# Three kernels in one program: where scratch stores, weight loads and token groups stand in the order

## Chip, cores and metric

One core of one Trainium2 chip. The metric is the time of the whole program on the device in microseconds (us), median of several runs. The profile is of one execution, taken by the hardware profiler.

## What is computed

An attention with a learned position bias, then a mixture of experts with one expert per token, then a gated feed-forward layer; 4 batches of 576 tokens, model width 512. Cut to what matters here:

```python
# attention: 4 batches x 8 heads, 576 positions, 64 channels, bias from a small net of log distances
attn = softmax(q @ k.T / 8 + bias);  x = attn @ v                     # (2304, 512)
# experts: each token goes to the expert with the largest logit
e = argmax(x @ w_gate);  h = relu(x @ w1[e]);  x = gate * (h @ w2[e]) # 8 experts, 512 -> 1024 -> 512
# gated layer, 512 -> 1536 -> 512
g = x @ w_gate2;  out = (g * sigmoid(g) * (x @ w_val)) @ w_out
```

## The kernel before

All of it is one program, and the order of the instructions on each engine is written out by hand; an engine's queue, and SP's queue of DMA issues too, is worked off in order. Matmuls are done in pairs of halves (a high part and the rest), so every weight and every activation is split by a copy on ScalarE and a subtraction on VectorE.

The attention ends at about 300 us. Then come 64 steps, numbered 0 to 63, 16 for each batch: step s of a batch does one block of 128 hidden units for one half of the tokens (the loop over `16 * B`, L1161). A step n issues on TensorE the first product of step n + 1 (`h_step`, L590, followed by a relu on ScalarE, L592, and a difference on VectorE, L593) and then the second product of step n (`y_step`, L603). So the relu of a step has about one step of time before TensorE needs it. After these two come all tasks noted for step n: `at(n, ...)` puts a task in the list `todo[n]`, `after(n, ...)` one in `done[n]`, and `todo[n]` is issued before `done[n]`.

The tasks that matter here:

- **Expert weights.** A batch b, from 1 on, has n = 16b - 15 as its base. Its expert's eight blocks come in three loads (`m_load`, `load_w`, L534 for w1 and L535 for w2) at steps n + 7, n + 8 and n + 11, that is 8, 9, 12 for batch 1, 24, 25, 28 for batch 2 and 40, 41, 44 for batch 3. The first two hold three blocks each, 768 KB for w1 and 768 KB for w2. `m_conv` splits block f at step n + 9 + f (`conv_w`, L551 on ScalarE, L553 on VectorE): block 0 at 10, 26 and 42.
- **Pieces of the last layer's weights.** The weights of the last layer lie in HBM as 64-bit numbers. A piece of them is fetched (`fetch_w`, L974 and L976, 512 KB), made 32-bit by one pass on ScalarE (L985) and three on VectorE (L988, L991, L994), and stored to the scratch tensor `wn` in HBM (L1031, 256 KB). 18 such pieces are done in the steps of the list `NS`. Piece i is fetched three steps before its own (`stash_ld`), into one of three buffers, and converted into one of two halves of `xT2`: `s_out(i)` is the half i % 2. So a piece may be converted only when the store of piece i - 2 has left. The steps of `NS2` divide a conversion over two steps. The store is noted by `after` for the step behind the conversion.
- **Batch list.** At steps 39 to 42 small products sort what is left over (`rest_list`, L516 the last), and 43 to 63 prepare one small extra group of tokens.

The last layer, from about 570 us, takes 36 iterations: three token groups j (768 tokens each, 384 and 384 side by side), and for each 12 blocks f of 128 hidden units, the middle group backwards. Iteration n does products for block f into the banks X and Y (L1276 in the first six iterations, L1267 after), VectorE's and ScalarE's work between, and the output product of iteration n - 1 (`outs`, L1529). In iterations 1 to 5 further pieces of weights are converted (`n_tasks`, L985 to L994, store L1413) and fetched again (`n_load`). Group j's x is read by `ld_x(j)` (L1468, and for the last group also L1479, whose rows are 128 bytes) into the tile `xr`, and its sums (L1233) are made by VectorE: those of the first read in iterations 3 and 4, those of the others in the third and second last iteration of the group before. `ld_x(0)` stands at the end of iteration 2, `ld_x(1)` at the end of iteration 7 and `ld_x(2)` at the end of iteration 18. Group 0 and group 1 are parts of the first three batches in an order known at run time; group 2 is the last batch and the last 64 tokens of each batch, whose outputs are stored in pieces of 32 rows. At the end of a group the six output tiles are copied (VectorE for m = 0 and 2, ScalarE for m = 1, the last tile half and half) and stored (L1548). In the last group the stores of m = 1, and half of the 32-row stores, are issued by ScalarE's queue, the others by SP.

Of the kernel before, what the change touches and what calls it, by code (L numbers as in the profile page):

```python
# [9 lines left out]
F32 = mybir.dt.float32  # L10
# [25 lines left out]
PR = {0: 72, 1: 73, 5: 75}  # L36
EB = 4
N0, NPL = 6, 6
NS = (9, 10, 13, 18, 19, 20, 21, 24, 25, 26, 29, 34, 35, 37, 39, 40, 41, 43)
NS2 = (13, 29, 37, 43)  # L40
RT = (3, 4, 5, 5, 6, 7, 7)
QN = (43, 46, 44, 46, 49, 54, 56)
# [71 lines left out]
def body(tc, qt, kt, va, vb, ws, moe_w_gate, moe_w_output_gate, moe_w1, moe_w2, w_gate, w_val, w_out, ctab, cst, cst2, out):  # L114
    nc = tc.nc
    with ExitStack() as ctx:
# [4 lines left out]
        vw = ctx.enter_context(tc.tile_pool(name="vw", bufs=1))  # L121
# [34 lines left out]
        for r in range(4):  # L156
            o = slice(32 * r, 32 * r + 32)
# [9 lines left out]
        vt = {}  # L167
# [594 lines left out]
        mu = [dict(raw=[], ws={}, xs={}) for b in range(B)]  # L762
# [3 lines left out]
        def m_load(b, gi):  # L766
            if gi == 0:
                mu[b]["e"] = nc.values_load(e0i[0:1, b:b + 1], engines=[ENG.SP], min_val=0, max_val=7)
            mu[b]["raw"] += load_w(mu[b]["e"], gi, "rv" if (b, gi) == (0, 1) else "vt")

        def m_load_f(b, f):

# [103 lines left out]
        for cnt in range(Z0):  # L876
            z_iter()
            n = -(-len(extra) // (Z0 - cnt))
# [13 lines left out]
        for n, (ui, c) in enumerate(steps):  # L892
            p, b = units[ui]
# [120 lines left out]
        def s_out(i):  # L1014
            return xT[2][:, 512 * (i % 2):512 * (i % 2) + 512]

        def stash(i, n, m, two):

            def cv(k, e):
                for f in fs()[k:e]:  # L1020
                    f()
            fl = []

            def fs():
                if not fl:
                    fl.extend(narrow_w(s_raw(i), s_out(i)))
                return fl
            at(m, lambda: cv(0, 4 if not two else 3))
            if two:
                at(m + 1, lambda: cv(3, 4))  # L1030
            after(m + 1 + two, lambda: nc.sync.dma_start(wn[n], s_out(i)))  # L1031

        def stash_ld(i, n, m):
            at(m - 3, lambda: fetch_w(n, s_raw(i)))
# [3 lines left out]
        def after(n, *fs):  # L1038
            done.setdefault(n, []).extend(fs)
# [327 lines left out]
        with ExitStack() as c2:  # L1367
# [152 lines left out]
            def outs(n, h, m):  # L1520
                j, f = steps[n]
                first, last = n % NF == 0, n % NF == NF - 1
                if first:
                    ops[h, m] = po.tile([128, 512], F32, tag=f"o{h}{m}", name="o")
                t = ops[h, m]
                uh, ul = (u[:, 128 * m:128 * m + 128] for u in sv[n]["u"][h])
                oh, ol = wt[f][2]
                for i, (u, w) in enumerate(((uh, oh), (uh, ol), (ul, oh))):
                    nc.tensor.matmul(t, u, w, start=first and i == 0, stop=last and i == 2)  # L1529
                if last:  # L1530
                    end = j == 2
                    if end:
                        o = sv["end"][:, 512 * (3 * h + m):512 * (3 * h + m) + 512]
                    else:
                        o = wp.tile([128, DM], F32, tag="ot", bufs=3, name="ot")
                    parts = rows(j, h, m)
                    if end and (h, m) == (1, 2):
                        nc.vector.tensor_copy(o[:, 0:256], t[:, 0:256])
                        nc.scalar.activation(o[:, 256:512], t[:, 256:512], AF.Copy)
                        nc.sync.dma_start(parts[0][2][:, 0:256], o[:, 0:256])  # L1540
                        nc.scalar.dma_start(parts[0][2][:, 256:512], o[:, 256:512])
                        return
                    if m % 2 == 0:
                        nc.vector.tensor_copy(o, t)
                    else:
                        nc.scalar.activation(o, t, AF.Copy)
                    for a, c, dst in parts:
                        (nc.scalar if end and (m % 2 or a >= 64) else nc.sync).dma_start(dst, o[a:a + c])  # L1548

            def it(n):  # L1550

# [28 lines left out]
                if n < NPL:  # L1580
                    st_new(n, X, Y, {t: wp.tile([128, TH], F32, tag=t, bufs=2, name=t) for t in ("c1", "c2")})
                    s = sv[n]
                    F("a")
                    plain(0, 0, f, X)
                    p_silu(s, 0)
                    F("b")
                    O(0, 0)
                    plain(0, 1, f, Y)
                    p_mul(s, 0)
                    u_hi(s, 0)  # L1590
                    F("c")
                    u_lo(s, 0)
                    O(0, 1)
                    O(0, 2)
                    F("d")
                    plain(1, 0, f, X)
                    p_silu(s, 1)
                    F("e")
                    O(1, 0)
                    O(1, 1)  # L1600
                    F("f")
                    plain(1, 1, f, Y)
                    p_mul(s, 1)
                    u_hi(s, 1)
                    F("g")
                    u_lo(s, 1)
                    O(1, 2)
                    F("h")
                    if i == 2:
                        ld_x(0)  # L1610
                    return
                st_new(n, X, Y, {t: wp.tile([128, TH], F32, tag=t, bufs=1 + (t[0] == "c"), name=t) for t in ("x1", "u2", "u4", "c1", "c2", "c3")})
# [36 lines left out]
                F("h")  # L1649
                O(1, 2)  # L1650
                if j < 2 and i == NPL + (j == 0):
                    ld_x(j + 1)

            for n in range(6, 9):
                n_load(n)
# [23 lines left out]
```

## Time and profile before

| | us |
|---|---|
| median of 3 runs | 1004.45 |
| lowest and highest | 1001.57, 1006.0 |
| the profiled execution, own time | 1007.01 |
| its span, first to last instruction | 1005.1 |

Busy time is the time in which an engine executed; TensorE's matmuls overlap, so a busy TensorE is not one at its peak, and the count of matmuls in a stretch says more. The granted clock is the share of full speed that TensorE got: 1.00 is 2.4 GHz, 0.5 is 1.2 GHz. In a timeline each row has start, duration, engine, line, operation, output and inputs, and how often it came; in square brackets stands the idle time before it and what ended it. SPq and ACTq are the queues of DMA issues; their durations are those of issuing, not of moving bytes.

### The profile page before, as it was taken

What the parts mean: (1) busy time and instruction counts of PE and PEld (TensorE: products, weight loads), DVE (VectorE), ACT (ScalarE), POOL (GpSimd) and SP (SyncE); (2) the same over time, 40 slices, a digit from 0 to 9 for tenths busy, and PEclk for the clock granted to TensorE, in tenths of its full rate; (3) what the DMA queues carried; (4) which work ended last, traced back from release to release, by engine and by line L of the source; (5) the groups of instructions that cost most, each with busy time, mean ns of one, the idle gap of its engine ahead of it and who ended that gap; (6) DMA issues with size and microseconds to landing.
All of it is one profiled execution on the core that took longest, in us unless ns stands there. A gap on an engine that the chain in (4) does not pass through costs nothing. (4 is left out here: it accounts for less than half of the span.)

```text
span 1005.1 us, 19647 instructions
## 1 busy us (share of the span) xinstructions
PE 959.9 (96%) x7633; PEld 819.7 (82%) x7633; DVE 694.7 (69%) x1548; ACT 531.3 (53%) x1125; POOL 115.8 (12%) x116
## 2 busy tenths in 40 slices
PE   7979999999999999797999998999999999999997
PEld 2337777777668999796999897999999999999996
DVE  8967788777786576574656666867636677556673
ACT  6767777777775252341434542554534554444542
POOL 2673333343300000000000000000000000000000
PEclk9998999999999999798999999999999999999999
DMA  6774324333044465766646367241122420302211
GB/s 205 206 247 151 117 86 151 99 116 111 2 141 155 158 232 160 257 198 215 203 163 214 131 211 240 94 127 32 41 86 64 126 63 1 126 32 63 64 32 63
DMA packets 88639, 130.26 MB, mean 130 GB/s; under 512 B 13632, under 2 KB 46400, under 8 KB 88544
## 3 DMA queue, kind: packets, MB, share of 16 engines
q1 hardware_dynamic: 87920, 128.07, 40.2%
q8 instruction: 60, 0.98, 0.4%
q10 hardware_dynamic: 624, 0.92, 0.3%
q14 instruction: 35, 0.29, 0.1%
HBM read 93.50 MB, written 35.46 MB: 128 GB/s over the span
## 5 line engine op out<-in xcount | busy, mean ns | idle before, releaser
L272 DVE CUSTOM_DVE_ANT_0 E<-S,bias 128x576 f32<-128x576 f32 x128 | 91.8, 755 | 34.8 <-PE S L268 26.5
L277 ACT ACTIVATE E<-E,st 128x576 f32<-128x576 f32 x144 | 110.3, 769 | 4.2 <-DVE st L272 3.9
L1267 PE MATMUL Y<-fv,ws 128*128 128x384 f32 x540 | 108.8, 336 | 0.0
L1267 PEld LDWEIGHTS Y<-fv,ws 128*128 128x128 f32 x540 | 95.7, 188 | 3.0 <-issue 0.2
L268 PEld LDWEIGHTS S<-kh,qz 64*128 64x128 f32 (+1 forms) x576 | 57.7, 189 | 38.7 <-DVE st L272 21.0
L379 PE MATMUL pv<-pt,rawv 128*64 128x320 f32 (+1 forms) x576 | 88.1, 423 | 0.0
L268 PE MATMUL S<-kh,qz 64*128 64x288 f32 (+1 forms) x576 | 83.9, 326 | 4.0 <-DVE st L272 2.6
L1529 PE MATMUL o<-ws,u 128*128 128x512 f32 x306 | 84.2, 395 | 0.0
L592 ACT ACTIVATE qz<-T 128x288 fp32r<-128x288 f32 x63 | 25.8, 409 | 94.7 <-PE T L590 94.5
L1008 DVE TENSOR_TENSOR ws<-r,ws 128x512 fp32r<-128x512 f32 (+1 forms) x66 | 51.4, 779 | 31.9 <-ACT ws L1005 30.9
L1267 PE MATMUL X<-fr,ws 128*128 128x384 f32 x360 | 73.4, 339 | 0.0
L318 ACT ACTIVATE pt<-T 128x512 f32<-128x512 f32 (+3 forms) x112 | 50.7, 467 | 40.4 <-PE T L295 40.0
L1267 PEld LDWEIGHTS X<-fr,ws 128*128 128x128 f32 x360 | 65.0, 188 | 5.6
L603 PE MATMUL y<-qz,w2hl 128*128 128x288 f32 x384 | 58.7, 302 | 8.6 <-ACT qz L592 6.1
L603 PEld LDWEIGHTS y<-qz,w2hl 128*128 128x128 f32 x384 | 54.3, 193 | 10.3 <-ACT qz L592 7.8
L1529 PEld LDWEIGHTS o<-ws,u 128*128 128x128 f32 x306 | 56.2, 188 | 6.6 <-DVE u L1322 0.4
L590 PE MATMUL T<-xh,whl 128*128 128x288 f32 x256 | 58.1, 303 | 0.0
L320 DVE COPY pt<-T 128x512 f32<-128x512 f32 (+3 forms) x112 | 55.8, 521 | 3.3 <-PE T L295 3.1
L593 DVE SCALAR_TENSOR_TENSOR qz<-T,qz 128x288 fp32r<-128x288 f32 x63 | 28.7, 455 | 42.0 <-ACT qz L592 41.4
L590 PE MATMUL T<-xh,w1hl 128*128 128x288 f32 x248 | 56.9, 305 | 0.0
L603 PE MATMUL y<-qz,whl 128*128 128x288 f32 x384 | 56.5, 296 | 0.0
L295 PE MATMUL T<-ident,E 64*128 64x64 f32 x1248 | 55.3, 225 | 0.0
(314 smaller groups left out, 2131.5 us busy)
## 6 DMA issues: line engine op xcount, KB each, us to landing
raww<-in_moe_w_dram SPq DMA_DIRECT2D x16, 768.0 KB, 7.3
r<-wn SPq DMA_DIRECT2D x22, 512.0 KB, 3.7
bscr<-ob SPq DMA_DIRECT2D x36, 288.0 KB, 3.3
bias<-bscr SPq DMA_DIRECT2D x14, 576.0 KB, 4.2
ro<-wn SPq DMA_DIRECT2D x22, 256.0 KB, 2.7
rawq<-in_qt_dram SPq DMA_DIRECT2D x16, 320.0 KB, 2.9
rawk<-in_kt_dram SPq DMA_DIRECT2D x16, 288.0 KB, 3.5
x<-xT SPq DMA_DIRECT2D x16, 288.0 KB, 4.8
```

The costliest lines, as they stand in the source:

```text
L268: nc.tensor.matmul(t[:, f, 0:288], x[k, a], y[k, o], start=i == 0, stop=i == 2)
L272: nc.vector.tensor_tensor_reduce(out=E.rearrange("p (a b) -> p a b", a=2), in0=ps[:, :, 0:288], in1=bt[p, hh, c].rearrange("p (a b) -> p a ...
L277: nc.scalar.activation(E, E, AF.Exp, bias=st[:, 2 * c + hh:2 * c + hh + 1], scale=-1.0, accum_out=st[:, 10 + 2 * c + hh:11 + 2 * c + hh])
L295: nc.tensor.transpose(t[r][:, at:at + 64], E[k, o:o + 128], ident[k, k])
L318: nc.scalar.activation(o, x, AF.Copy)
L320: nc.vector.tensor_copy(o, x)
L379: nc.tensor.matmul(st["ps"][64 * hh:64 * hh + 64, 0:w], vt[p][:, hh, b, c, :], y, start=c == order[0], stop=c == order[4])
L590: nc.tensor.matmul(ps, wa[:, x, k], xs[k][y][:, o], start=k == 0 and i == 0, stop=k == 3 and i == 2)
L603: nc.tensor.matmul(hbuf["y"][d // 2][:, d % 2, 0:288], wb[:, x, d], t[:, y:y + 288], start=f == 0 and i == 0, stop=(one or f == 7) and i == 2)
L1008: return lambda: eng.tensor_tensor(l, t, h.bitcast(F32), ALU.subtract)
L1267: nc.tensor.matmul(bank, a[:, c], x[:, k], start=first and k == 0 and n == 0, stop=k == 1 and n == 2, skip_group_check=True)
L1529: nc.tensor.matmul(t, u, w, start=first and i == 0, stop=last and i == 2)
```

## The change

Five edits. In `NS` the piece at step 26 is taken out and one at 49 is added, so that the pieces from the tenth on move to the next later place of the list. A piece's store is noted for the step in which its conversion ends, not for the one after. A batch's first weight load is issued as block 0 of w1 and of w2, and then blocks 1 and 2 of each. `ld_x(0)` stands at the end of iteration 1. The second and third group of tokens change places: the group with the 32-row pieces is loaded second and stored at iteration 24, and the whole blocks come last; all of the last stores are issued by SP.

```diff
-NS = (9, 10, 13, 18, 19, 20, 21, 24, 25, 26, 29, 34, 35, 37, 39, 40, 41, 43)
+NS = (9, 10, 13, 18, 19, 20, 21, 24, 25, 29, 34, 35, 37, 39, 40, 41, 43, 49)
@@ m_load
             if gi == 0:
                 mu[b]["e"] = nc.values_load(e0i[0:1, b:b + 1], engines=[ENG.SP], min_val=0, max_val=7)
-            mu[b]["raw"] += load_w(mu[b]["e"], gi, "rv" if (b, gi) == (0, 1) else "vt")
+                t, e = vw.tile([128, 3072], F32, tag="vt", bufs=2, name="raww"), mu[b]["e"]
+                a = t[:, 0:1536].rearrange("p (k f) -> p k f", k=4)
+                c = t[:, 1536:3072].rearrange("p (f d) -> p f d", f=3)
+                for i, j in ((0, 1), (1, 3)):
+                    nc.sync.dma_start(a[:, :, 128 * i:128 * j], moe_w1[bass.ds(e, 1), :, 128 * i:128 * j].rearrange("o (k p) f -> p (o k) f", p=128))
+                    nc.sync.dma_start(c[:, i:j], moe_w2[bass.ds(e, 1), 128 * i:128 * j].rearrange("o (f p) d -> p (o f) d", p=128))
+                mu[b]["raw"] += [(a[:, :, 128 * i:128 * i + 128], c[:, i]) for i in range(3)]
+            else:
+                mu[b]["raw"] += load_w(mu[b]["e"], gi, "rv" if (b, gi) == (0, 1) else "vt")
@@ stash
-            after(m + 1 + two, lambda: nc.sync.dma_start(wn[n], s_out(i)))
+            after(m + two, lambda: nc.sync.dma_start(wn[n], s_out(i)))
@@ outs
-                    parts = rows(j, h, m)
+                    parts = rows((0, 2, 1)[j], h, m)
                     if end and (h, m) == (1, 2):
...
-                        nc.scalar.dma_start(parts[0][2][:, 256:512], o[:, 256:512])
+                        nc.sync.dma_start(parts[0][2][:, 256:512], o[:, 256:512])
...
-                        (nc.scalar if end and (m % 2 or a >= 64) else nc.sync).dma_start(dst, o[a:a + c])
+                        nc.sync.dma_start(dst, o[a:a + c])
@@ it
-                    if i == 2:
+                    if i == 1:
                         ld_x(0)
...
-                    ld_x(j + 1)
+                    ld_x(2 - j)
```

## Rows read from the trace of the kernel before

**Rows 1.** The page, busy us and share of the span: TensorE.
```profile
PE 959.9 (96%) x7633; PEld 819.7 (82%) x7633; DVE 694.7 (69%) x1548; ACT 531.3 (53%) x1125; POOL 115.8 (12%) x116
```
**Rows 2.** Stretches: us, busy time (instructions) per engine, granted clock, DMA share, GB/s.
```profile
340.00:360.00 20.00, 18.68 (x139) 18.23 (x138) 13.15 (x24) 9.44 (x19) 0.00 (x0) 1.00 0.77 264
360.00:400.00 40.00, 40.00 (x318) 38.69 (x317) 30.04 (x73) 15.43 (x34) 0.11 (x1) 1.00 0.57 178
400.00:420.00 20.00, 13.31 (x76) 12.75 (x76) 7.07 (x14) 5.85 (x13) 0.00 (x0) 0.74 0.84 296
460.00:480.00 20.00, 13.04 (x92) 12.55 (x92) 7.84 (x26) 4.43 (x9) 0.00 (x0) 0.83 0.66 215
570.00:610.00 40.00, 40.00 (x220) 37.96 (x219) 27.11 (x48) 16.97 (x32) 0.00 (x0) 1.00 0.68 222
610.00:630.00 20.00, 15.94 (x75) 14.39 (x75) 12.19 (x20) 6.03 (x12) 0.00 (x0) 0.91 0.65 210
630.00:990.00 360.00, 360.00 (x1873) 334.99 (x1872) 237.66 (x431) 169.79 (x327) 0.00 (x0) 1.00 0.22 66
```
**Rows 3.** Timeline of TensorE, 398 to 412: second products of three steps.
```profile
398.77 1.74 PE L603 MATMUL y<-qz,w2hl 128*128 128x288 f32 x12
...
401.95 1.75 PE L603 MATMUL y<-qz,w2hl 128*128 128x288 f32 x12
...
410.44 0.61 PE L603 MATMUL y<-qz,w2hl 128*128 128x288 f32 x1 [5.14 <-ACT qz L592]
```
**Rows 4.** Timeline of ScalarE, two conversions of pieces.
```profile
408.39 0.66 ACT L985 ACTIVATE xT<-xT 128x512 f32<-128x512 f32 x1 [9.02 <-DMA wn<-xT]
...
469.29 0.66 ACT L985 ACTIVATE xT<-xT 128x512 f32<-128x512 f32 x1 [8.13 <-DMA wn<-xT]
```
**Rows 5.** Timeline of SP's queue, 395 to 412: batch 2's loads, a store.
```profile
396.38 0.41 SPq L534 DMA_DIRECT2D raww<-in_moe_w_dram  x1
...
397.60 0.37 SPq L534 DMA_DIRECT2D raww<-in_moe_w_dram  x1
...
399.44 0.34 SPq L1031 DMA_DIRECT2D wn<-xT  x1
```
**Rows 6.** Timeline of SP's queue, 456 to 464: batch 3's loads, a store.
```profile
459.20 0.40 SPq L534 DMA_DIRECT2D raww<-in_moe_w_dram  x1
...
460.22 0.48 SPq L1031 DMA_DIRECT2D wn<-xT  x1
460.90 0.46 SPq L534 DMA_DIRECT2D raww<-in_moe_w_dram  x1
```
**Rows 7.** Timeline of ScalarE, 343 to 351: batch 1's first block.
```profile
346.14 0.63 ACT L551 ACTIVATE w1hl<-raww 128x512 fp32r<-128x512 f32 x1 [1.96 <-DMA raww<-in_moe_w_dram]
349.50 0.63 ACT L551 ACTIVATE w2hl<-raww 128x512 fp32r<-128x512 f32 x1 [2.73 <-DMA raww<-in_moe_w_dram]
```
**Rows 8.** DMA issues of the whole span: count, KB each, median us to landing.
```profile
raww<-in_moe_w_dram SPq DMA_DIRECT2D x16, 768.0 KB, 7.3
...
wn<-xT SPq DMA_DIRECT2D x18, 256.0 KB, 4.7
...
raww<-in_moe_w_dram SPq DMA_DIRECT2D x16, 256.0 KB, 4.6
```
**Rows 9.** Timeline of SP's queue, 591 to 609: a fetch, the x load.
```profile
592.10 0.42 SPq L976 DMA_DIRECT2D nr<-in_w_out_dram  x1
...
605.15 2.70 SPq L1468 DMA_DIRECT2D xr<-x  x4
```
**Rows 10.** Timeline of VectorE, 612 to 616: the first x sum.
```profile
614.08 0.96 DVE L1233 TENSOR_TENSOR sx<-xr 128x768 f32<-128x768 f32 x1 [5.48 <-DMA xr<-x]
```
**Rows 11.** Timeline of all engines, 986 to 1006: the last stores.
```profile
997.32 2.23 SPq L1548 DMA_DIRECT2D out_dram<-oend  x5
...
1000.48 0.60 ACT L1546 ACTIVATE oend<-o 128x512 f32<-128x512 f32 x1 [1.63 <-issue]
...
1001.92 0.36 ACTq L1541 DMA_DIRECT2D out_dram<-oend  x1
```

## Prediction

> **What bounds the kernel now.** I read the page's busy times first. TensorE is busy for 959.9 of 1005.1 us [rows 1], so only the 45 us in which it stands, and whatever it runs at the lower clock, can be won by moving transfers about. The table of stretches, read next, says where. In 360 to 400 TensorE is busy throughout at granted clock 1.00 and retires 318 matmuls in 40 us, 7.9 per us; in 570 to 610 it retires 220, 5.5 per us; from 630 to 990 it never stands [rows 2]. Four stretches of 20 us between fall short of these rates. Missing matmuls divided by the rate give the time lost, idle and lower clock together:
> - 340 to 360: 139 of 158, 2.4 us
> - 400 to 420: 76 of 158, 10.4 us, clock 0.74
> - 460 to 480: 92 of 158, 8.4 us, clock 0.83
> - 610 to 630: 75 of 110, 6.4 us, clock 0.91
>
> Together 27.6 us. Then the engines' timelines were read at these four places for what ends the wait.
>
> At 400 TensorE's steps follow each other by 3.18 us (398.77 to 401.95); the next y step, due at 405.1, starts at 410.44 because ScalarE's relu is late [rows 3]. ScalarE is late because a piece's conversion (L985) sat 9.02 us before 408.39 for a store to wn, and 8.13 us before 469.29 for another [rows 4]. The piece writes the half of xT2 that the piece two before it wrote, and may not until that one's store has left. That store was issued at 399.44, behind both weight loads of the batch (issued from 396.38 and 397.60) [rows 5], in the second case at 460.22, between the two [rows 6]: a 256 KB store which usually lands after 4.7 us [rows 8] took 9.0 (399.44 to 408.39) and 9.1 (460.22 to 469.29). After each, TensorE is granted 1.2 GHz for a time: 0.74 over 20 us is 10.4 us at half of 2.4 GHz.
>
> At 346 ScalarE waits 1.96 and 2.73 us for the raw weights of a batch's first block [rows 7]. At 614 VectorE waits 5.48 us for the x rows [rows 10], whose load was issued at 605.15 [rows 9].
>
> **The change part by part.**
>
> *Piece 26 goes to 49, the others shift.* Steps 24, 25, 26 become 24, 25, 29: the piece that needs the half of the piece at 24 now comes five steps (16 us at 3.18) after it, not two. The store had 9.0 us to go from its issue in the worst case; even so it is done. The 10.4 us of 400 to 420 go; I take 10.0, as the lookahead of one step that the next wait eats is not free (bounds 8.0 to 10.4). Added at 49 is the same work of one piece: a fetch of 512 KB three steps before, one ScalarE pass of 0.66 us as in [rows 4], three VectorE passes, one store. TensorE's steps hide it where ScalarE is 15.4 of 40 us busy [rows 2]; without that cover it would cost about 2.5 us. I put 0.2 (0 to 2.5).
>
> *Stores in their own step.* After it, steps 39, 40, 41 keep three pieces in a row, so 41 still needs 39's half. Before, 39's store was in SP's list of step 40 behind the batch's first load [rows 6]; now it stands in step 39 ahead of it. From the fetch-and-load group's start at 459.2 it gains at least 1.0 us of issue and, above all, 1.5 MB of loads no longer lie in front of it. At the median 4.7 us [rows 8] from about 458 it lands at 462.7, against ScalarE's arrival at 469.29 - 8.13 = 461.2: a wait of 1.5 us at most, within one step. What is late next is 40's store, now behind the first load, for the piece at 43; if it again takes 9.1 us from about 462 it lands at 471, and ScalarE arrives about 468. Of these 3 us one step of 3.2 covers all or nearly all. I take 8.0 of 8.4 (bounds 6.0 to 8.4). The store now waits on SP for VectorE's last pass of its own step, and SP's later DMAs (next step's fetch and loads) queue behind that. In [rows 5] the store followed the loads with no gap, so its data were ready; other stores just come earlier: 0, bounds 0 to 1.
>
> *First blocks alone.* A batch's first load (two DMAs of 768 KB) becomes four: block 0 (2 x 256 KB), then blocks 1 and 2 (2 x 512 KB). By the median, a 256 KB load of these weights lands 4.6 us after issue, a 768 KB one 7.3 [rows 8]. In batch 1 ScalarE reached block 0 at 346.14 - 1.96 = 344.2; issued at about 341 it lands at 345.5, so of 4.7 us waiting 1.3 stay, under one step: the 2.4 us of 340 to 360 go but for 0.5, 1.9 won (bounds 0 to 2.4). In batch 2 this part is needed, not a gain: with piece 26 gone ScalarE reaches block 0 at about 399.4 (the relu behind the matmuls that end as y starts at 398.77 [rows 3]), three us after the issue at 396.38 [rows 5]; 4.6 us later is 401.0, 1.6 us of waiting, covered, where a 768 KB load at 7.3 would keep it to 404.3 and hold the relu due at 402. Blocks 1 and 2 are issued 1.2 us later and are wanted one step later. SP issues two DMAs more per batch, 0.6 us each (396.38 to 397.60 is two), with nothing urgent behind: 0.5 us in all (0 to 2). Here the Trainium skill speaks against the change: "DMA: Bandwidth & Descriptors", section Bandwidth (Measured), wants transfers batched to 1 MiB or more and, in the section Anatomy of one DMA, puts about 2.0 us fixed on each (for DMAs that GpSimd issues); taken in series, two more DMAs would bring blocks 1 and 2 some 4 us later, 0.8 beyond a step in each of three batches, an estimate of 2.4 us more. The rows show 256 KB loads landing 2.7 us sooner than 768 KB ones, issued 0.6 us apart, so the fixed part overlaps; I stay with the rows.
>
> *x read a step sooner.* The first x load moves from the end of iteration 2 to that of iteration 1, behind the fetch at 592.10 [rows 9], 12.5 us sooner. All that it reads is stored before this loop begins, so it is issued at about 592.6 and, taking as long as before (605.15 to 614.08 is 8.9 us), is in by 601.5, 7 us before VectorE's sum at 608.6. The 6.4 us go, with the lower clock after them; I take 6.0 (4.5 to 6.4), as VectorE afterwards has little spare. The 1.5 MB stand in front of the next iteration's fetches, which are wanted most of an iteration after their issue: 0 to 0.5.
>
> *Order of the token groups.* The group with the 128-byte x rows is loaded at iteration 7 instead of 18 and needed two or three iterations later either way; both lie in 630 to 990, where TensorE is busy for 360.00 of 360 us and DMA for 0.22 [rows 2], so there is room: 0. At the very end ScalarE issues stores between its copies: a copy starts at 1000.48 after 1.63 us of nothing but issuing, and the last store leaves at 1001.92 [rows 11]. With whole blocks there are 7 issues instead of 13, all on SP; SP took 2.23 us for five from 997.32 [rows 11], so seven of 0.45 to 0.6 us, each behind its copy, end at 1000.5 to 1001.5. I take 0.8 us (-0.5 to 1.4: seven issues in a row on one queue can also end later than two queues did, and the bytes are the same).
>
> **Sum.** 10.0 + 8.0 + 1.9 + 6.0 + 0.8 = 26.7 won, 0.2 + 0.5 + 0.5 for held relus of batches 2 and 3 spent: 25.5 us. The profiled execution took 1007.01 us (span 1005.1), 2.6 above the median of 1004.45; its parts would give 981.5, the median less the same 25.5 gives 979. The waits are for landings, which differ between runs, so part of the 2.6 may lie in the very waits that go. I take 979.
>
> **The rivals.** *The blocks are not told apart*: block 0's conversion waits for the whole load. For it: blocks 1 and 2 are interleaved with block 0 in the tile's columns. Against: the x load writes interleaved columns in one tile by four DMAs issued within 2.7 us [rows 9]. Price: 1.9 of batch 1, and in batch 2 a relu held from 402 to about 404.5: 2.5; 25.5 - 4.4 = 21.1, so 983.5. *Batch 3's wait only shifts* from step 41 to 43 because the DMA engines are full there anyway: 8.0 lost, 987. *Both stores' waits become waits for weights*: the 3 MB of two loads take to 408 in any case, and ScalarE stands for them instead of for the store. Against: blocks are wanted in order, one per 3.2 us, not all at once. It would leave 7.5 us of gain, 997, at worst no change. *Slower*: SP held by stores. Each store now keeps SP until VectorE is done with that piece, and in batches 2 and 3 the second load stands behind one (the pieces at 24 and 40). In batch 2 that load was issued from 397.60 on, right after the first, and its first block is wanted at step 29, three steps after 398.77, about 408.4; landing in 7.3 us leaves 3.5, and the lookahead 3.2 more. From a hold of 6.7 us it decides, and what lies beyond appears one for one, with some 5 us of lower clock behind it as at 400 to 420. Holds of 17 us would cost 15 in each of two batches, 30 against 25.5: 1009. The row at 399.44 speaks against any hold.
>
> **How the numbers follow.** Forecast 0.76, blocks 0.09, batch 3 0.08, weights 0.04, slower 0.03. All bounds at their best win 29.0, 975.4; all at their worst win 18.0 and spend 6.0, 992. The range 974.5 to 988 takes in the first three cases (0.93) and leaves out only many worst ends at once. 0.5% is 5 us, about what a measurement here can tell from no change: faster 0.94, same 0.03, slower 0.03.
>
> **What would show it.** Right: in the table of stretches the same places busy throughout at clock 1.00; no ScalarE wait for wn<-xT over 3 us; block 0's wait under 2 us; no VectorE wait for xr; no ScalarE issuing in the tail. Wrong: a new wait for raww at the second load, a conversion at 43 that waits over 4 us, or SP standing at L1031 in front of a load.

## The result

| kernel | median us | lowest to highest | ratio to before, 95% interval |
|---|---|---|---|
| before | 1004.05 (4 runs) | 1001.57 to 1006.0 | |
| changed | 996.1 (4 runs) | 994.33 to 996.33 | 0.9918 [0.9893, 0.9943] |

The change wins 8 us, not the 25.5 that were forecast, and the time lies 8 us above the range; it is above the 992 too that the prediction gave for all its bounds at their worst. The profiled execution of the changed kernel took 994.33 us, the fastest of its four; its span is 992.4.

First the table of stretches of the changed kernel, which answers to [rows 2]; the columns are the same.

```profile
340.00:360.00 20.00, 20.00 (x153) 20.00 (x152) 15.30 (x30) 10.85 (x22) 0.00 (x0) 1.00 0.77 269
400.00:420.00 20.00, 19.74 (x149) 19.50 (x148) 14.35 (x28) 10.02 (x21) 0.00 (x0) 1.00 1.03 373
460.00:480.00 20.00, 18.23 (x137) 17.76 (x136) 12.40 (x31) 5.55 (x12) 0.00 (x0) 1.00 0.71 236
480.00:520.00 40.00, 36.47 (x256) 34.54 (x254) 20.95 (x41) 15.34 (x33) 0.00 (x0) 0.96 0.49 163
...
610.00:630.00 20.00, 20.00 (x105) 18.45 (x104) 17.81 (x32) 10.88 (x20) 0.00 (x0) 1.00 0.29 102
...
980.00:992.40 12.40, 0.00 (x0) 0.00 (x0) 0.00 (x0) 0.00 (x0) 0.00 (x0) 0.53 0.27 98
```

The stands that the prediction wanted gone are gone: 340 to 360 went from 139 to 153 matmuls, 400 to 420 from 76 to 149, 610 to 630 from 75 to 105, and 460 to 480 from 92 to 137, where a smaller stand at step 46 is left. But the last line is new: for over 12 us at the end no engine computes, and the transfer engines are used to 0.27. A smaller hole stands between 480 and 520.

The length of a step n, here and below, is the time from the start of its second product (L603) to that of step n + 1. By these starts and the end of the last matmul the two spans, 1005.1 and 992.4, differ like this:

| stretch | before to after, us |
|---|---|
| up to the first step's second product (305.19, 301.32) | -3.9 |
| steps 0 to 45: 11 and 12 from 4.27 and 3.96 to 3.19 each, 27 and 28 from 8.49 and 7.84 to 3.19 each, 31 from 3.20 to 3.73, 42 from 12.69 to 4.01 | -20.1 |
| steps 46 to 52: 46 from 3.61 to 5.23, 49 to 51 from 3.63, 3.64, 3.65 to 4.28, 4.98, 7.30 | +7.3 |
| last layer and the loops ahead of it, to the end of the last matmul | -3.9 |
| from the last matmul to the end of the span (6.3, 14.2) | +7.9 |

The first line isn't the change's: in 60 to 80 TensorE was granted 0.76 in the profiled execution of before and 1.00 in that of after, over work that is the same. Without it the two spans differ by 8.8 us, near the 8 of the medians. In the fourth, the wait for x at 614 and its lower clock are gone (6.4 by [rows 2]), and 1 to 2 us come back between 535 and 575, where the granted clock is 0.96 (0.04 of 40 us is 1.6).

The end, in the timeline of SP's queue after, and in TensorE's (its last group of products); [rows 11] show it before:

```profile
976.73 9.04 SPq L1556 DMA_DIRECT2D out_dram<-oend  x5
987.63 0.33 SPq L1548 DMA_DIRECT2D out_dram<-oend  x1
989.60 0.33 SPq L1549 DMA_DIRECT2D out_dram<-oend  x1
```

```profile
973.74 4.50 PE L1537 MATMUL o<-ws,u 128*128 128x512 f32 x18
```

And the waits of SP's queue over the same stretch (us in total, times, longest):

```profile
SPq L1556 <- DMA out_dram<-oend: 6.5, 4, 1.6
SPq L1548 <- DMA out_dram<-oend: 1.6, 1, 1.6
SPq L1549 <- DMA out_dram<-oend: 1.4, 1, 1.4
```

TensorE ends at 978.24 and the span at 992.4. The seven stores leave one every 2.15 us (976.73 to 989.60 is six intervals), for each but the first waits some 1.6 us until the store before it has landed. Before, five stores of the last group left in 2.23 us.

The profile of before had shown this chain, in a place where it cost nothing. At the end of its second group, the one that the change moves to the end, at 859, SP's queue and its waits are:

```profile
859.13 11.54 SPq L1548 DMA_DIRECT2D out_dram<-ot  x6
```

```profile
SPq L1548 <- DMA out_dram<-ot: 8.3, 5, 1.7
```

Six stores, five waits for landing, 11.54 us; the six of the first group, at 720, look the same (11.44 us, 8.1 of it in five waits). There TensorE goes on with the next group, so nobody felt it. The first two groups are the ones whose rows have run-time places in the output (`bass.ds(r0, 1)` and its like); the group that stood last before the change has fixed ones. The change put a group of the first kind where the end of the span waits for it.

The second new hole, at steps 46 to 51, is in the timelines of SP's queue, ScalarE, VectorE and TensorE:

```profile
467.89 2.48 SPq L638 DMA_DIRECT2D qz<-x  x4
470.41 0.43 SPq L984 DMA_DIRECT2D xT<-in_w_out_dram  x1
470.94 0.40 SPq L1142 DMA_DIRECT2D x<-yo  x1
```

```profile
480.68 0.60 ACT L667 ACTIVATE tok<-qps 128x512 f32<-128x512 f32 x1 [6.10 <-DMA x<-yo]
481.17 0.66 ACT L993 ACTIVATE xT<-xT 128x512 f32<-128x512 f32 x1
481.72 1.14 ACT L551 ACTIVATE whl<-raww 128x512 fp32r<-128x512 f32 x2
482.76 0.40 ACT L592 ACTIVATE qz<-T 128x288 fp32r<-128x288 f32 x1
```

```profile
460.75 0.23 DVE L644 TENSOR_SCALAR meta<-meta,vm 128x5 f32<-128x5 f32 x1 [3.64 <-DMA meta<-gscr]
...
481.86 0.43 DVE L996 TENSOR_SCALAR xT<-xT 128x512 int32<-128x512 int32 x1 [6.80 <-ACT xT L993]
482.32 0.69 DVE L999 SCALAR_TENSOR_TENSOR xT<-xT,xT 128x512 int32<-128x512 int32 x1
483.05 0.69 DVE L1002 SCALAR_TENSOR_TENSOR xT<-xT,xT 128x512 int32<-128x512 int32 x1
483.66 1.29 DVE L553 TENSOR_TENSOR whl<-raww,whl 128x512 fp32r<-128x512 f32 x2
484.87 0.81 DVE L593 SCALAR_TENSOR_TENSOR qz<-T,qz 128x288 fp32r<-128x288 f32 x2
```

```profile
483.22 0.40 PE L603 MATMUL y<-qz,w2hl 128*128 128x288 f32 x1 [1.18 <-ACT qz L592]
485.37 2.73 PE L603 MATMUL y<-qz,w2hl 128*128 128x288 f32 x11 [1.75 <-DVE qz L593]
```

Read from the bottom: TensorE waits for the relu's second half (L593), which VectorE does at 484.87 behind three passes of a piece (L996 to L1002) and a weight split. ScalarE had come to these late, because at step 49 it copies the first tokens of the small extra group (`tok`) into the buffer from which batch 2's output (`yo`, 1152 KB) is still being stored: both are the one buffer of the tag `rv`. That store was issued at 470.94, directly behind the fetch of the piece now converted at step 49 (470.41, 512 KB). The profile of before had a row of this wait too; there it was 2.16 us, and no piece stood behind it:

```profile
499.10 0.60 ACT L667 ACTIVATE tok<-qps 128x512 f32<-128x512 f32 x1 [2.16 <-DMA x<-yo]
```

A third, small one is step 31 (3.20 to 3.73). ScalarE's conversion of the piece at step 29 now waits for that piece's own fetch, which before had the long steps 27 and 28 to land in:

```profile
406.12 0.66 ACT L993 ACTIVATE xT<-xT 128x512 f32<-128x512 f32 x1 [2.82 <-DMA xT<-in_w_gate_dram]
```

This wait is not the same in every execution: it is 4.35 to 4.88 us in three of the profiles below (groups taken back, x later, piece fetched early), and steps 30 and 31 together then take 8.4 to 10.3 us, where they take 6.9 here and 6.5 with both repairs.

### The profile page after: what moved, and what is told of

The parts are those of the page before. It is cut to its first block, busy times and chain, and to the rows that moved or that the text cites. A ratio compares the mean times of both kernels' runs of the same rounds, so it can differ in the third digit from the quotient of the medians.

```text
span 992.4 us, 19678 instructions
## 1 busy us (share of the span) xinstructions
PE 953.1 (96%) x7633; PEld 813.4 (82%) x7633; DVE 694.2 (70%) x1548; ACT 532.0 (54%) x1125; POOL 115.9 (12%) x116
## 5 line engine op out<-in xcount | busy, mean ns | idle before, releaser
L603 PE MATMUL y<-qz,w2hl 128*128 128x288 f32 x384 | 57.8, 300 | 3.5 <-DVE qz L593 1.7
L603 PE MATMUL y<-qz,whl 128*128 128x288 f32 x384 | 56.9, 296 | 1.6 <-DVE qz L593 1.6
L603 PEld LDWEIGHTS y<-qz,w2hl 128*128 128x128 f32 x384 | 53.7, 191 | 4.7 <-ACT qz L592 2.7
L603 PEld LDWEIGHTS y<-qz,whl 128*128 128x128 f32 x384 | 52.8, 188 | 2.1 <-DVE qz L593 2.1
```

What stands on the lines that cost most here:

```text
L603: nc.tensor.matmul(hbuf["y"][d // 2][:, d % 2, 0:288], wb[:, x, d], t[:, y:y + 288], start=f == 0 and i == 0, stop=(one or f == 7) and i == 2)
```

## Experiments

Two theories were put to the test first: the end is long because stores with run-time places wait for each other, and steps 49 to 51 are long because of the piece put there. In the table every kernel ran beside the kernel before on the same chip; the last three columns are of its profiled execution. "Both" stands for the kernel with both repairs.

| kernel | median us | lowest to highest | ratio to before, 95% | span | last matmul ends | between |
|---|---|---|---|---|---|---|
| groups taken back | 986.47 | 983.35 to 990.88 | 0.9812 [0.9771, 0.9852] | 989.0 | 981.69 | 7.3 |
| two queues | 993.5 | 991.98 to 995.27 | 0.9898 [0.9862, 0.9934] | 990.1 | 975.70 | 14.4 |
| piece at 16 | 991.13 | 990.37 to 992.66 | 0.9873 [0.9839, 0.9908] | 988.5 | | |
| both repairs | 981.21 | 980.68 to 982.4 | 0.9774 [0.974, 0.9807] | 978.8 | 972.73 | 6.1 |
| fixed places | 987.21 | 983.0 to 992.39 | 0.9844 [0.9799, 0.9889] | 982.8 | 977.64 | 5.2 |
| both, VectorE's keep later | 980.87 | 979.15 to 982.69 | 0.9775 [0.9758, 0.9792] | 977.2 | | |
| both, stores late | 988.11 | 987.37 to 990.34 | 0.9844 [0.9823, 0.9865] | 986.9 | | |
| both, piece at 26 | 987.36 | 983.92 to 990.68 | 0.9822 [0.98, 0.9845] | 988.8 | | |
| both, whole blocks | 981.72 | 981.11 to 982.75 | 0.9776 [0.9758, 0.9795] | 979.6 | | |
| both, x later | 988.16 | 987.61 to 988.64 | 0.9838 [0.982, 0.9855] | 986.4 | | |
| repaired end, piece at 49 fetched early | 983.3 | 980.95 to 984.46 | 0.9782 [0.976, 0.9804] | 982.6 | | |
| one store less | 993.89 | 989.49 to 995.54 | 0.9881 [0.9847, 0.9914] | 993.6 | 981.27 | 12.3 |

The kernel before had medians of 1006.32, 1004.2 and 1004.65 us beside the first four rows, the second four and the last four, so times of different fours are comparable to some 2 us only.

### Order of the token groups taken back

```
-                    parts = rows((0, 2, 1)[j], h, m)
+                    parts = rows(j, h, m)
-                    ld_x(2 - j)
+                    ld_x(j + 1)
```

> The changed kernel with its order of token groups taken back (rows go to the output, and x to its tile, in the order of the kernel before, so that the last six products belong to batch 3 and to the tail rows, whose places in the output are fixed); all stores stay on SP's queue. Theory, run-time addresses: a store whose place in the output is known only at run time waits until the store before it has landed, about 2.05 us each, and in the changed kernel the last seven are of that kind. With fixed places SP has no such waits: the span ends about 6 to 7 us behind the last matmul (14.1 us in the changed kernel) and the time is about 988 us (996.1 less 7.5). Rival, one queue: the stores wait because all of them stand on SP's queue. Then the 13 stores of this kernel wait too, 12 times 2.05 us, and the span ends over 20 us behind the last matmul, at about 1003 us or more.

986.47 us. Thirteen stores on one queue, 32-row ones among them, and no chain; SP's queue:

```profile
980.18 5.10 SPq L1556 DMA_DIRECT2D out_dram<-oend  x11
985.38 0.40 SPq L1548 DMA_DIRECT2D out_dram<-oend  x1
985.87 0.41 SPq L1549 DMA_DIRECT2D out_dram<-oend  x1
```

Eleven issues in 5.10 us, where five took 9.04, and the span ends 7.3 us behind the last matmul. So it is not the one queue. Of the 9.6 us that the time falls, 6.9 are this end (14.2 to 7.3); what the rest is this run doesn't tell.

### The last stores shared over two queues

```
-        at(QR, lambda: ... engines=[ENG.SP], ...
+        at(QR, lambda: ... engines=[ENG.SP, ENG.Activation], ...
...
-                        nc.sync.dma_start(dst, o[a:a + c])
+                        (nc.scalar if end and (m % 2 or a >= 64) else nc.sync).dma_start(dst, o[a:a + c])
```

(QR is where the run-time places are loaded; the last half store is on ScalarE's queue too)

> The changed kernel with its order of token groups kept, but the last stores shared between SP's and ScalarE's queues as in the kernel before (the run-time addresses are loaded on ScalarE as well). Theory, run-time addresses: the stores wait for each other across queues, because what they wait for is the landing of the store before; the span still ends 12 to 15 us behind the last matmul and the time stays within 2 us of 996.1 us. Rival, one queue: with three or four stores on each queue the chain is half as long, the span ends 7 to 9 us behind the last matmul, and the time is about 990 us.

993.5 us, 14.4 us of end. ScalarE's timeline, and SP's queue:

```profile
976.36 0.39 ACTq L1556 DMA_DIRECT2D out_dram<-oend  x1
976.80 0.60 ACT L1554 ACTIVATE oend<-o 128x512 f32<-128x512 f32 x1 [3.20 <-DMA out_dram<-oend]
983.04 0.34 ACTq L1556 DMA_DIRECT2D out_dram<-oend  x1
983.42 0.38 ACT L1547 ACTIVATE oend<-o 128x256 f32<-128x256 f32 x1 [6.02 <-DMA out_dram<-oend]
987.25 0.34 ACTq L1549 DMA_DIRECT2D out_dram<-oend  x1
```

```profile
974.18 7.02 SPq L1556 DMA_DIRECT2D out_dram<-oend  x3
985.26 0.33 SPq L1548 DMA_DIRECT2D out_dram<-oend  x1
```

The chain goes through both queues: a store on SP waits for one of ScalarE's and the other way round, 974.18 to 987.25 is six intervals of 2.18 us. It also holds ScalarE's copies, which stand behind its stores. The time is 2.6 us below the changed kernel's, a little more than the 2 us that were allowed; the end is no part of that, but in its profiled execution steps 49 to 51 take 13.5 us together, not 16.6.

### Fixed places

```
-                    parts = rows((0, 2, 1)[j], h, m)
+                    parts = rows((0, 2, 1)[j], h, m, (0, 1, 2))
             def rows(j, h, m, at):
+                r0, r1, r2 = at
```

> The changed kernel with one thing replaced: the places of the output rows of the three chosen batches are constants (batches 0, 1, 2) in place of the values read at run time; order of the token groups, loads of x and queue of the stores are kept. So some rows may stand at another batch's place than the reference has them; the amount of work is the same. Theory, run-time addresses: the six chained stores of the end go, the span ends 6 to 7.5 us behind the last matmul and the time is 988 to 990 us against 996.1. Rival, order of the groups: the end is long because of what the last group is, whatever its addresses; then it stays at 12 to 14 us and the time at 994 to 997 us.

987.21 us. SP's queue:

```profile
976.13 2.40 SPq L1557 DMA_DIRECT2D out_dram<-oend  x5
978.63 0.59 SPq L1549 DMA_DIRECT2D out_dram<-oend  x1
979.31 0.59 SPq L1550 DMA_DIRECT2D out_dram<-oend  x1
```

The kernel writes the three batches to fixed places, whatever their order; the work is the same. Same group, same bytes, same queue; with constants for the places the five leave in 2.40 us, not 9.04, and the span ends 5.2 us behind the last matmul. The end is 9.0 us shorter and the time falls by 8.9, a little more than expected. The run-time places alone make the chain.

The first group's stores, in the middle of the kernel, lose their waits for landing too, but still take 9.60 us (11.41 in the changed kernel):

```profile
699.30 9.60 SPq L1557 DMA_DIRECT2D out_dram<-ot  x6
```

SP waits there for the copies that fill the tiles. So the 11.5 us of such a row in the middle are not the price of the chain; the price is in its waits for landing. Why a run-time place makes a store wait is inferred, not shown: places that aren't known beforehand can't be told apart, so the built program keeps writes to the one output tensor in order.

### One store less

```
-                        nc.sync.dma_start(parts[0][2][:, 0:256], o[:, 0:256])
-                        nc.sync.dma_start(parts[0][2][:, 256:512], o[:, 256:512])
+                        nc.sync.dma_start(parts[0][2], o)
```

> The changed kernel with its last two half stores (columns 0 to 255 and 256 to 511 of the same 128 rows) made one store, behind the same two copies. Theory, each store in the chain waits a landing: one link less, the span ends 12 to 12.3 us behind the last matmul instead of 14.1 us and the time falls by 1.8 to 2.1 us, to about 994.2 us. Rival, bytes: the chain is as long as its bytes take to be written; these are the same, the end stays at 14 us and the time at 996 us.

993.89 us and 12.3 us of end: one link less, 1.9 us less, with the same bytes. So the price goes by the number of stores, not by the bytes.

### The piece of step 49 put at 16

```
-NS = (9, 10, 13, 18, 19, 20, 21, 24, 25, 29, 34, 35, 37, 39, 40, 41, 43, 49)
+NS = (9, 10, 13, 16, 18, 19, 20, 21, 24, 25, 29, 34, 35, 37, 39, 40, 41, 43)
```

> The changed kernel with its piece of step 49 put at step 16 instead, all else kept. Theory, the piece: steps 49 to 51 of the changed kernel are 4.28, 4.98 and 7.30 us long instead of 3.6 each, because the piece's fetch, its 3.2 us on ScalarE and its store stand between the late x rows and the work that waits for them. Without it these steps come back to about 3.6 us each, step 16 costs 0 to 1 us, and the time is 990 to 991.5 us (996.1 less 5.6, and up to 1 more). Rival, the rows themselves: the loads of x rows issued at 467.89 meet the queue of the weights that now come closer in time, and land at 480 whatever the piece does. Then steps 49 to 51 keep at least 4 us of their 5.6 and the time is 994.5 to 996.5 us.

991.13 us, 5.0 less. Steps 49 to 51 are 3.64, 3.61 and 3.80 us, and step 16 stays at 3.16. (The piece has 0.66 us on ScalarE and 1.8 on VectorE, not the 3.2 on ScalarE of the expectation.)

### Both repairs

The edits of "order of the token groups taken back" and "the piece of step 49 put at 16", and the last stores' queues as they were:

```
-                        nc.sync.dma_start(parts[0][2][:, 256:512], o[:, 256:512])
+                        nc.scalar.dma_start(parts[0][2][:, 256:512], o[:, 256:512])
-                        nc.sync.dma_start(dst, o[a:a + c])
+                        (nc.scalar if end and (m % 2 or a >= 64) else nc.sync).dma_start(dst, o[a:a + c])
```

> The changed kernel with its order of token groups and its split of the last stores over two queues taken back, and the piece of step 49 put at step 16. Theories of the run-time addresses and of the piece together: 996.1 less 7.9 (the tail of 14.1 us back to 6.25 us) less 5.6, and up to 1 for step 16: 982.5 to 984 us. If the piece is not what lengthens steps 49 to 51: about 988 us. If the tail comes from something else than the order of the groups: 990 us or more.

981.21 us, 23 us (2.3%) below the kernel before, 14.9 below the changed one and 1.3 below the range expected; the two repairs alone gave 9.6 and 5.0, together 14.6, so they add up. ScalarE's timeline at step 49:

```profile
479.50 0.60 ACT L667 ACTIVATE tok<-qps 128x512 f32<-128x512 f32 x1 [4.25 <-DMA x<-yo]
480.00 1.14 ACT L551 ACTIVATE whl<-raww 128x512 fp32r<-128x512 f32 x2
481.04 0.40 ACT L592 ACTIVATE qz<-T 128x288 fp32r<-128x288 f32 x1
```

The wait for batch 2's output is still there, 4.25 us, so the expectation for the piece at 16 was wrong to speak of late x rows. But ScalarE is released 4.9 us behind the start of step 49's second product (474.64), against 6.7 in the changed kernel (473.96 to 480.68), and no piece stands between the token copy and the work for the next relu.

### The piece kept at 49, fetched two steps sooner

```
-            at(m - 3, lambda: fetch_w(n, s_raw(i)))
+            at(m - 3 - 2 * (m == 49), lambda: fetch_w(n, s_raw(i)))
```

(with order and queues of the last stores taken back)

> The kernel with the order and queues of the last stores taken back, and the piece kept at step 49, but with its fetch of 512 KB issued two steps sooner, where the transfer engines are idle. It tells apart what the piece costs there: by its fetch, which goes ahead of batch 2's output of 1152 KB, on whose landing ScalarE waits before it may write the tokens over the same buffer; or by its 0.5 us on ScalarE and 1.8 us on VectorE between this wait and the next step's work. With the fetch as it was, both repairs less the piece's would give 986.2 us (981.21 and 5.0 more, the piece's cost between the changed kernel and the one with the piece at 16). Theory, fetch: about half of it, 1.9 us and the lower clock that follows, goes: 982 to 984 us. Rival, engines: nothing goes but 0.5 us at most: 985.5 to 986.5 us.

983.3 us. ScalarE's token copy now waits:

```profile
482.37 0.60 ACT L667 ACTIVATE tok<-qps 128x512 f32<-128x512 f32 x1 [2.84 <-DMA x<-yo]
```

It starts 3.5 us behind step 49's second product (478.92); steps 49 to 51 are 3.63, 3.64 and 4.49 us. So the fetch, 512 KB ahead of the output that ScalarE waits for, was the larger part of the piece's price, and its passes on ScalarE and VectorE the smaller one: 983.3 is 2.1 us above both repairs, 2.9 below the 986.2 that the piece with its old fetch would give. By the steps the fetch's part is larger still: 49 to 51 take 16.56 us together in the changed kernel, 11.76 here and 11.34 with both repairs, while steps 30 and 31, which the piece has no part in, are 2.4 us longer here than with both repairs. All profiles agree: in the five kernels with the fetch ahead of the output ScalarE is released 5.2 to 6.7 us behind step 49's second product and the three steps take 13.5 to 16.6 us; in the other nine, the kernel before among them, it is 2.3 to 4.9 and 10.9 to 11.8.

### VectorE's work on the routing weights a step later

```
-QN = (43, 46, 44, 46, 49, 54, 56)
+QN = (43, 46, 45, 46, 49, 54, 56)
```

> The kernel with both repairs (order and queues of the last stores taken back, piece at step 16; 981.21 us) with VectorE's work on the routing weights moved from step 44 to step 45, that is one step further behind the loads of these weights (4 bytes per packet) which it waits for. Theory: the wait goes, step 46 comes back from 4.76 us to 3.2 to 3.6 us and the time falls by 1.1 to 1.6 us, to about 980 us. Rival: the wait is only passed on to the next thing in this stretch (the x rows that step 50 waits for, which come a fixed time behind the loads); then steps 46 to 51 keep their sum of 22.5 us within 0.4 and the time stays at 981 us.

980.87 us. The wait at L644 was 2.68 us in the kernel with both repairs; VectorE's timeline there, and then here:

```profile
461.43 0.23 DVE L644 TENSOR_SCALAR meta<-meta,vm 128x5 f32<-128x5 f32 x1 [2.68 <-DMA meta<-gscr]
```

```profile
461.81 0.23 DVE L644 TENSOR_SCALAR meta<-meta,vm 128x5 f32<-128x5 f32 x1
```

Step 46 goes from 4.76 to 3.61 us and steps 49 to 51 don't grow (3.63, 3.64, 3.65). So the wait isn't passed on. In the time the 1.15 us can't be seen: ratios 0.9774 and 0.9775.

### Parts of the change undone, one at a time

A piece's store one step later again:

```
-            after(m + two, lambda: nc.sync.dma_start(wn[n], s_out(i)))
+            after(m + 1 + two, lambda: nc.sync.dma_start(wn[n], s_out(i)))
```

> The kernel with both repairs (981.21 us) with one part undone: a piece's store is issued one step behind its conversion again, as before the change. Theory of the prediction: SP then stands in front of batch 3's first weight load again, step 42 goes from 4.01 to about 12 us and the time rises by 8 to 8.7 us, to 989 to 990 us. Rival: what held batch 3 was the crowd of pieces that the other moves have thinned; then step 42 stays below 6 us and the time below 983.5 us.

988.11 us, 6.9 more, less than the 8 to 8.7 expected. Step 42 is 13.30 us long, not by SP standing in front of a load, as the expectation has it, but by a wait of ScalarE like the second of [rows 4]:

```profile
456.13 0.66 ACT L993 ACTIVATE xT<-xT 128x512 f32<-128x512 f32 x1 [8.75 <-DMA wn<-xT]
```

Step 46, behind this long one, is back at 3.61 us.

The piece at 26 again:

```
-NS = (9, 10, 13, 16, 18, 19, 20, 21, 24, 25, 29, 34, 35, 37, 39, 40, 41, 43)
+NS = (9, 10, 13, 18, 19, 20, 21, 24, 25, 26, 29, 34, 35, 37, 39, 40, 41, 43)
```

> The kernel with both repairs (981.21 us) with one part undone: the pieces stand at the steps of the kernel before, so that one is converted at step 26, directly behind those of 24 and 25, and none at 16. Theory of the prediction: the place of the piece is what made steps 27 and 28 long (8.49 and 7.84 us against 3.19), so they come back to 8 to 16 us together above 6.4, and the time rises by 8 to 10 us, to about 990 us. Rival: SP's queue made them long, by stores that stood ahead of the third piece's fetch; with the stores in their own step they stay below 4.5 us each and the time below 984 us.

987.36 us, 6.2 more (4.8 by the ratios), less than the 8 to 10 expected. Steps 27 and 28 are 5.77 and 7.84 us, 7.2 above two of 3.19, and ScalarE waits as in the first of [rows 4]:

```profile
402.43 0.66 ACT L993 ACTIVATE xT<-xT 128x512 f32<-128x512 f32 x1 [6.29 <-DMA wn<-xT]
```

Its wait was 9.02 us before: the store in its own step alone takes off 2.7, and moving the piece the rest.

The first blocks loaded with the others again:

```
-                for i, j in ((0, 1), (1, 3)):
...
-            else:
-                mu[b]["raw"] += load_w(mu[b]["e"], gi, "rv" if (b, gi) == (0, 1) else "vt")
+            mu[b]["raw"] += load_w(mu[b]["e"], gi, "rv" if (b, gi) == (0, 1) else "vt")
```

> The kernel with both repairs (981.21 us) with one part undone: the first weight blocks of a batch are loaded as one pair of loads of three blocks each again, not as one block and then two. Theory of the prediction: batch 1 waits again for its first block (steps 11 and 12, 4.27 and 3.96 us before against 3.19 now), 1.9 us, and batches 2 and 3 may each wait as much at steps 27 and 42, so 983 to 986 us. Rival: with SP free sooner the whole blocks also land in time; then these steps stay at their lengths and the time within 1 us of 981.2 us.

981.72 us, no difference, as the rival had it. ScalarE does wait for the whole load of batch 1:

```profile
344.98 0.63 ACT L551 ACTIVATE w1hl<-raww 128x512 fp32r<-128x512 f32 x1 [1.15 <-DMA raww<-in_moe_w_dram]
...
347.00 0.63 ACT L551 ACTIVATE w2hl<-raww 128x512 fp32r<-128x512 f32 x1 [1.39 <-DMA raww<-in_moe_w_dram]
```

But 1.15 and 1.39 us are within the lookahead of one step, and steps 11 and 12 keep their 3.19; only step 28 grows, from 3.19 to 3.57. In [rows 7] the same waits were 1.96 and 2.73 us.

The first group's x one step later again:

```
-                    if i == 1:
+                    if i == 2:
                         ld_x(0)
```

> The kernel with both repairs (981.21 us) with one part undone: the first group's x is loaded one step later again. Theory of the prediction: VectorE waits for the loads of x again (5.5 us before the change), work of TensorE stands behind it, and the time rises by 5 to 6 us, to 986 to 987.5 us. Rival: this wait came from SP's queue, which the other parts have emptied; then the time stays below 982.5 us.

988.16 us, 6.9 more (6.4 by the ratios), above the 5 to 6 expected. VectorE's wait of [rows 10] is back, within a tenth of a us:

```profile
595.45 0.96 DVE L1241 TENSOR_TENSOR sx<-xr 128x768 f32<-128x768 f32 x1 [5.46 <-DMA xr<-x]
```

From step 53 to the last matmul the profiled execution is 4.9 us longer than with both repairs. Another 2.0 are in steps 30 and 31, far ahead of x, and aren't x's.

## Why the prediction was wrong, and where it was right

**The tail: the term that decided.** The prediction gave the end +0.8 us, from "seven of 0.45 to 0.6 us" that it read from five stores with fixed places [rows 11]. It cost 7.9. The counting was not the fault: with fixed places the seven stores do end 5.2 us behind the last matmul, 1.1 better than the 6.3 of before. The fault was that the duration of one instruction was taken from a row of another kind. The group that comes to the end is stored at 859 in the kernel before, by the same line, and SP's waits there say five landings, 8.3 us. "The bytes are the same" was true and beside the point. Nor did the slower rival see it: it looked for SP held at the pieces' stores. SP does stand there (between 320 and 500 it waits 28.0 us in seven times at L1039 for VectorE, 6.1 at most), but of the steps 0 to 45 only step 31 is longer than before by more than 0.1 us.

**The piece at 49: second wrong term.** The prediction gave 0.2 us (0 to 2.5), because ScalarE is busy for 15.4 of 40 us [rows 2]. The piece costs 5.0. A mean share of a stretch elsewhere says nothing of a step where ScalarE stands in a wait, as it did at step 49 before (2.16 us); what delays the end of that wait is on the path. The piece's fetch was counted as work but not placed in its queue: it goes ahead of batch 2's output, for which ScalarE waits. The fetch is the larger part of the 5.0: 2.9 by the medians, more by the lengths of the steps.

**A wait that came nearer.** The rest of steps 46 to 51, 1.6 us at step 46, is neither of the two: the routing weights' loads, which before had the long step 42 to land in, are waited for once it is short, and no longer when it is long again (store one step later). The wait at step 31 is of the same kind. The prediction asked what is late next only as far as step 43.

**Right: four stands, and the causes of three.** All four went as forecast, and for three of them undoing the part shows that it was a reason: the store 6.9 us (forecast 8.0, bounds 6.0 to 8.4), the piece at 26 4.8 to 6.2 (forecast 10.0, bounds 8.0 to 10.4), x 6.4 to 6.9 in time and 4.9 in the stretch where x is read (forecast 6.0, bounds 4.5 to 6.4). The stand at 400 was worth the 10.0: steps 27 and 28 fell from 16.3 to 6.4 us. But the forecast gave all of it to the piece, and the store's move does part of the same work: ScalarE's wait falls by 2.7 without the piece's move, and 7.2 us of the two steps are left for it.

**The blocks: gain right by luck, reason wrong.** Steps 11 and 12 did shrink, by 1.9 us, but not by the split load: with whole blocks they are as short. The 1.9 us that the prediction gave to this part, less 0.5, were 0 to 0.5. What made batch 1's whole loads land sooner than before is open: SP issues them at the same place of the step in both (2.35 us ahead of the next second product's start), and in the kernel before one of the issues took 1.17 us, here 0.52. No run separated this from the stores' move. The rule of the Trainium skill against the split, "DMA: Bandwidth & Descriptors", section Bandwidth, isn't borne out either, nor is the estimate of 2.4 us lost that the prediction worked out beside it: with and without the split the ratio is 0.9774 and 0.9776.

Taken together: without the tail's 0.8 and the piece's -0.2 the prediction's sum is 24.9, which from 1004.45 gives 979.6; the kernel with both repairs, in which these two terms are nothing, takes 981.2. Of the 17 us by which the forecast was wrong, 14.9 go with the two repairs, of the end of the kernel and of step 49; the waits that came nearer are in what is left. The signs that the prediction named mostly came out right (no wait for wn<-xT over 1.2 us, none for xr, no store on ScalarE's queue at the end), and the time was wrong all the same: none of them asks how long the end is, or looks at step 49.

## What to carry to other kernels

Before work is moved to the end of a kernel, look up what the same work does where it stands now: a queue that waits 1.6 us for each landing costs nothing in the middle and full price at the end. Price an added task by what stands ahead of it and behind it in each in-order queue of that very step, not by an engine's mean share. When waits are taken away, follow the transfers that had been landing under them for some steps on.

## What the hardware showed beyond that

A store of 128 rows to HBM whose successor has to wait for it costs 2.15 to 2.18 us from issue to next issue, on one queue or across two, and the half as large last ones hardly less (987.63 to 989.60 is 1.97). The Trainium skill has a fixed part of this size for DMAs that GpSimd issues, "DMA: Bandwidth & Descriptors", section Anatomy of one DMA: about 2.0 us, most of it until the write to memory is confirmed. This case's rows, of SP and ScalarE, agree in the size and in that bytes matter little, but lie below what the page's fit adds for the bytes (an estimate by it: 2.6 us for 256 KB, 2.3 for 128 KB).

Two profiles differ by some us where the kernels don't. The first step's second product starts at 305.19 us before, at 302.97 with both repairs and at 301.32 in the changed kernel, over work that is the same; in 60 to 80 TensorE was granted 0.76, 0.91 and 1.00. Between 535 and 575 the changed kernel was granted 0.96 and, after the same waits of the same length, the one with both repairs 1.00 (531 to 571 there). Why the clock falls in one and not in the other these runs don't show. The stands differ too, as at steps 30 and 31. The kernel with the groups taken back took 983.35 us at a mean granted clock of 0.998 and 990.88 at 0.989; only the second was profiled, so whether longer stands or the clock behind them made the difference is open.
